# Pooled attention and maxout layers: almost all products by seven, with attention, folds and loads in one written order

## The chip, the cores and the metric

One core of a Trainium2 chip runs the whole program. The metric is the device time of one execution in microseconds (us), the median of several runs. PE is the matmul engine, DVE the vector engine, ACT the scalar engine, POOL is GpSimd, SP the engine that here only issues DMAs.

## The reference, cut to what matters

```python
# q, k, v: (8 batches, 8 heads, 576 tokens, 64)
k_p = k.reshape(B, H, 72, 8, D).mean(axis=3)          # groups of 8 keys are averaged
v_p = v.reshape(B, H, 72, 8, D).mean(axis=3)
attn = softmax(q @ k_p.T / 8)
x = (attn @ v_p) as (4608 tokens, 512)
h = max(x @ w1, x @ w2, x @ w3)                       # w1..w3: 512 x 768
out = h @ w_out                                       # w_out: 768 x 512, float32
```

Attention goes by batches (576 tokens), the layers behind it by tiles of 512 tokens, n = 0 to 8, so that a tile needs tokens of two batches.

## The kernel before, in words

**Mathematics.** Only differences from w1 are multiplied: w2-w1 and w3-w1 replace w2 and w3 (`sub_w`), and max(x w1, x w2, x w3) = x w1 + max(0, x(w2-w1), x(w3-w1)). So a tile's output is x @ wm + h @ w_out, with wm = w1 @ w_out made once (`linear`) and h = max(0, x(w2-w1), x(w3-w1)). In a normal tile the first layers (`hidden`, `hidden_part`) are 6 blocks x 2 weights x 4 pieces, 48 matmuls of 512 columns, and the output (`project`) is 4 x 10 matmuls of 512.

**By seven.** A product of 2 x 2 blocks can be had from seven block products instead of eight, with sums of blocks on both sides (Strassen's scheme in Winograd's form). `seven` does it for first layers, `out_seven` for outputs. The weights' sums (`fold_w`, `fold_out`) are made once. The sums of the tokens (T1 to T4, `fold_x`, `sums_of`) and of h (`fold_h`, `sums_of`) are made for each tile. The products are added up partly in PSUM, partly by additions on DVE after ACT has copied a product out. First layers by seven are 84 matmuls of 256 columns, outputs by seven 70 of 256. Before, tiles 6 to 8 have first layers by seven, and tiles 2, 3, 4, 7 and 8 outputs by seven; the others are normal.

**Order.** Every engine works through its instructions in the order in which the program writes them (the scheduler is switched off). Up to the end of `linear` the order is that of `block(0, ...)`: attention of batch 0, tile 0's first layers, wm. Then come project(0), tiles 1 to 4, each from a word list in `MIDDLE` (h is a piece of the first layers, a digit a product of an output, k, q, s, v, x the attention steps of the next batch), tile 5 (`block(5, LEAD, ...)`), and a woven last part, `ORDER`, with batch 7, tiles 6 to 8 and the outputs of 5 and 6 (F). `s` makes scores and their exponentials, `v` multiplies by the values and divides, `x` turns the result into xT, the layers' operand: on PE up to batch 2, by a DMA transpose from SP from batch 3 on. `T` turns a batch's q by one DMA transpose into qT.

**Folds and loads.** The sums over eight keys or values of batches 1 to 7 (but batch 1's keys, which DVE folds) are made by POOL in three steps (`fold_steps`, L161, L162, L164), and loads of k, q, v (576 KB each in the tile's type) are issued in POOL's queue. Two buffers each hold kt, vt and qb. xT is a ring of 2048 tokens.

**PSUM** has eight banks. In the middle part three are pw (first layers, outputs), two pairs are att (attention), one is tr. In the woven part there are pa, bc, po, sc and val.

Of the kernel before, what the change touches and what calls it, by code (L numbers as in the profile page):

```python
# [14 lines left out]
def kernel(  # L15
# [26 lines left out]
    NG = 9  # L42
# [22 lines left out]
    kts, vts, qbs, kps, qTs, ets = {}, {}, {}, {}, {}, {}  # L65

# [15 lines left out]
    def load_v(b, eng, dtype=F16, cuts=(0, H)):  # L82
        if b == 0:
            vts[0] = ld.tile([96, 4096], dtype, name="vt0", tag="vt")[:, 0:3072].rearrange(
                "p (h i d) -> p h i d", h=H, i=6)
            src = v[0].rearrange("h (p i) d -> p h i d", i=6)
            return [eng.dma_start(out=vts[0][:, h:g], in_=src[:, h:g])
                    for h, g in zip(cuts, cuts[1:])][-1]
        vts[b] = ld.tile([Sp, H, POOL, D], dtype, name="vt", tag="vt")
        src = v[b].rearrange("h (sp j) d -> sp h j d", j=POOL)  # L90
        return [eng.dma_start(out=vts[b][:, h:g], in_=src[:, h:g])
                for h, g in zip(cuts, cuts[1:])][-1]

    def load_q(b):
        qbs[b] = ld.tile([128, 4, NG, D], BF16, name="qb", tag="qb")
        src = q[b].rearrange("h s d -> (h s d)").rearrange(
            "(hp p t d) -> p hp t d", hp=4, p=128, t=NG)
        n = 2 if b == 0 else 4
        for i in range(0, 4, n):
            nc.gpsimd.dma_start(out=qbs[b][:, i:i + n], in_=src[:, i:i + n])  # L100
# [42 lines left out]
    vp_all = const.tile([Sp, B, H, 65], F16, name="vp", tag="vp")  # L143
# [10 lines left out]
    def fold(e, t, out, dtype=F32):  # L154
        return list(fold_steps(e, t, out, dtype))

    def fold_steps(e, t, out, dtype=F32):
        part, n = t.shape[:2]
        f = const.tile([part, n, 4, D], dtype, name="half" if dtype == F32 else "halfh",
                       tag="half" if dtype == F32 else "k16")  # L160
        yield e.tensor_tensor(out=f, in0=t[:, :, 0:4, :], in1=t[:, :, 4:8, :], op=ALU.add)  # L161
        yield e.tensor_tensor(out=f[:, :, 0:2, :], in0=f[:, :, 0:2, :],  # L162
                              in1=f[:, :, 2:4, :], op=ALU.add)
        yield e.tensor_tensor(out=out, in0=f[:, :, 0, :], in1=f[:, :, 1, :], op=ALU.add)  # L164

    def new_kp(b):
        kps[b] = sb2.tile([96, 6, D], BF16, name="kp", tag="kp")

    def fold_k(b, e, i0=0, i1=6):
        if b not in kps:  # L170
            new_kp(b)
        fold(e, kts[b][:, i0:i1], kps[b][:, i0:i1], F16 if e is nc.vector else F32)

    def fold_v(b):
        fold(nc.gpsimd, vts[b], vp_all[:, b, :, 0:D])

    def pool_v(b, h, g, tag, evac):

        pvp = psum([128, g - h, D], F32, name="pvp", tag=tag[0], bufs=tag[1])
        for i in range(6):  # L180
            nc.tensor.matmul(pvp, pick[:, i, :], vts[b][:, h:g, i, :],
                             start=(i == 0), stop=(i == 5))
        evac(out=vp_all[:, b, h:g, 0:D], in_=pvp[0:Sp])

    def turn_q(b, n0, n1, evac, tag):
# [5 lines left out]
        for n in range(n0, n1):  # L191
            nc.tensor.transpose(pqt[:, n - n0, :], qf[:, 128 * n:128 * n + 128],
# [3 lines left out]
    def keys(b, tag):  # L196
        pkt = psum([128, 3, 96], BF16, name="pkt", tag=tag[0], bufs=tag[1])
        for i in range(3):
            nc.tensor.transpose(pkt[:, i, :],
                                kps[b][:, 2 * i:2 * i + 2, :].rearrange("p i d -> p (i d)"),  # L200
                                ident[0:96, 0:96])
        return pkt

    def turn_k(b):
        pkt = keys(b, ATT if len(pools) < 3 else SC)
        for par, evac in enumerate((nc.vector.tensor_copy, nc.scalar.copy)):
            for odd in range(2):
                (evac if b > 2 else nc.vector.tensor_copy)(
# [4 lines left out]
    def score(b, h, out, tp, i0, i1):  # L213
# [4 lines left out]
        nc.tensor.matmul(out, kz_all[b % 2][f % 2][rows, h, :],  # L218
# [28 lines left out]
    def turn_x(b, c0, keep, xn, tag, evac=nc.scalar.copy):  # L247
        g0 = S * b + c0
        if b > 2:
            cut = 128 - (g0 + 128) % RING  # L250
            cuts = (keep, cut, 128) if keep < cut < 128 else (keep, 128)
            for a, z in zip(cuts, cuts[1:]):
                nc.sync.dma_start_transpose(
                    out=tokens(g0 + a, g0 + z),
                    in_=xn.rearrange("p g h d -> p (g h d)")[a:z])
            return
        pxt = psum([128, KCH, 128], F16, name="pxt", tag=tag[0], bufs=tag[1])
        for kc in range(KCH):
            nc.tensor.transpose(
# [4 lines left out]
    def values(b, c0):  # L264
        tag = (ATT0, ATT, ("val", 1))[len(pools) - 1]
        pav = psum([128, 2, 512], F32, name="pav", tag=tag[0], bufs=tag[1])
        for h in range(H):
            nc.tensor.matmul(  # L268
                pav[:, h // 4, 65 * (h % 4):65 * (h % 4) + 65],
                ets[b][:, h, c0:c0 + 128], vp_all[:, b, h, :],  # L270
# [18 lines left out]
    xns, mms = {}, []  # L289

    def do(b, steps):
# [3 lines left out]
        for name in steps.split():  # L295
            i = int(name[1:] or 0)
            if name[0] in "qQ":
                turn_q(b, *QS[i], nc.vector.tensor_copy if name[0] == "Q"
                       else nc.scalar.copy, TR)
            elif name[0] == "T":  # L300
                qTs[b] = sb2.tile([128, 2 * NG, 128], BF16, name="qT", tag="qT")
                nc.sync.dma_start_transpose(
                    out=qTs[b], in_=qbs[b].rearrange("p hp t d -> p (hp t d)"))
            elif name[0] == "k":
                turn_k(b)
            elif name[0] == "K":
                fold_k(b, nc.vector)
# [7 lines left out]
            elif name[0] == "S":  # L315
                next(out_sums, None)
# [7 lines left out]
            else:  # L324
                turn_x(b, *CHUNKS[i], xns[b, i], TR if b == 1 else ATT,
                       nc.vector.tensor_copy if name[0] == "X" else nc.scalar.copy)
# [11 lines left out]
    def turn_w(jc, evac):  # L338
        pwt = psum([128, KCH, 128], F16, name="pwt", tag=TR[0], bufs=TR[1])
        for kc in range(KCH):  # L340
            nc.tensor.transpose(pwt[:, kc, :], w_sb[0][:, kc, bass.ts(jc, 128)], identh)
        evac(out=w1T[:, jc, :], in_=pwt.rearrange("p k c -> p (k c)"))

    def linear():

        for kc in range(KCH):
            pm = psum([128, C], F32, name="pm", tag="pw", bufs=3)
            for jc in range(JCH):
                nc.tensor.matmul(pm, w1T[:, jc, bass.ts(kc, 128)], wo_sb[:, jc, :],
# [7 lines left out]
    def hidden_part(n, jc, c0, c1, hT):  # L357
        x = tokens(NB * n + c0, NB * n + c1)
        for wi in range(1, 3):
            pw = psum([128, c1 - c0], F32, name=f"pw{wi}", tag="pw", bufs=3)  # L360
            for kc in range(KCH):
                mm = nc.tensor.matmul(pw, w_sb[wi][:, kc, bass.ts(jc, 128)],  # L362
# [37 lines left out]
    def project(n):  # L400
        hT = hTs[n]
        for mm in range(4):
            m = 4 * n + mm
            last = m == TOK // 128 - 9
# [3 lines left out]
            for c in ((slice(0, C // 2), slice(C // 2, C)) if last else (slice(0, C),)):  # L408
                tag = PW if len(pools) < 3 else PA if last else PO
                po = psum([128, c.stop - c.start], F32, name="po", tag=tag[0], bufs=tag[1])  # L410
                for kc in range(KCH):
                    nc.tensor.matmul(po, tokens(128 * m, 128 * m + 128)[:, kc], wm_sb[:, kc, c],  # L412
                                     start=(kc == 0), stop=False)
                yield
                for jc in (0, 3, 1, 4, 2, 5):
                    nc.tensor.matmul(po, hT[:, jc, bass.ts(mm, 128)], wo_sb[:, jc, c],  # L416
                                     start=False, stop=(jc == JCH - 1))
                if c.start:
                    nc.vector.tensor_copy(out=osb[:, c], in_=po)
                else:  # L420
                    nc.scalar.copy(out=osb[:, c], in_=po)  # L421
                for u in range(2):
                    b, g = divmod(2 * m + u, NG)
                    dst = out[S * b:S * b + S, :].rearrange("(r g) c -> r g c", g=NG)
                    (nc.scalar if last and u else nc.sync).dma_start(
                        out=dst[:, GS[g], c], in_=osb[64 * u:64 * u + 64, c])
# [5 lines left out]
    def heat(n):  # L432
        for _ in range(n):
            nc.tensor.matmul(wm, warm[:, 0:128], warm, start=True, stop=True)
# [12 lines left out]
    def sum_k0(a, i):  # L447
        for j in range(4):
            nc.tensor.matmul(pk0[a][:, i % 3], k16[:, i, j, :], identh[0:96, 0:96],
# [67 lines left out]
    def block(n, plan, parts):  # L517

        for slot, _ in enumerate(part for stage in parts for part in stage(n)):
            for b, steps in plan.get(slot, ()):  # L520
                if b < B:
                    do(b, steps)
# [3 lines left out]
    PA, BC, PO = ("pa", 2), ("bc", 1), ("po", 1)  # L526
    FIRST = {1: (0, 0), 2: (1, 2), 7: ("S3", "T3")}
    PRODUCTS = FIRST | {3: ("S4", 3), 4: (3, "T4"), 5: ("S1", "T1"), 6: ("S2", "T2")}
    sw = {}

    LEAD = {0: [(6, "s0")], 1: [(6, "s1")], 2: [(6, "s2")], 3: [(6, "s3")],
            4: [(6, "s4")], 5: [(6, "s5")], 6: [(6, "s6")], 7: [(6, "s7")],
            8: [(6, "v0 x0")], 9: [(6, "v1 x1")]}

    def minus(out, a, b):
        gate[:] = [nc.vector.tensor_tensor(out=out, in0=a, in1=b, op=ALU.subtract)]

    def fold_w(wi):
# [3 lines left out]
        tag = ("w1T", "mw0")[wi - 1]  # L542
        s = const.tile([128, 4, 2, 128 * JH], F16, name=f"sw{wi}", tag=tag)
        sw[wi] = dict(zip(range(4), a)) | {f"S{i + 1}": s[:, i] for i in range(4)}
        nc.vector.tensor_tensor(out=s[:, 0], in0=a[2], in1=a[3], op=ALU.add)
        yield
        minus(s[:, 2], a[0], a[2])
        yield
        minus(s[:, 1], s[:, 0], a[0])
        yield  # L550
        minus(s[:, 3], a[1], s[:, 1])
        yield

    def halves(n):

        return {i: tokens(NB * n + HALF * (i % 2), NB * n + HALF * (i % 2) + HALF,
                          2 * (i // 2), 2 * (i // 2) + 2) for i in range(4)}

    def turns(n):
        return (pad3 if n % 2 else pad)[:, 0:4]  # L560

    def fold_t(e, x, t):
        for i, a, b in ((0, x[1], x[0]), (1, x[3], t[0]), (2, x[3], x[1]), (3, x[2], t[1])):
            e.tensor_tensor(out=t[i], in0=a, in1=b, op=ALU.subtract)  # L564

    def fold_x(n):

        x, t = halves(n), turns(n)
        late = n >= LAST - 1
        for part in ([slice(0, 1), slice(1, 2)] if late else [slice(0, 2)]):  # L570
            fold_t(nc.gpsimd if late else nc.vector,
                   {i: x[i][:, part] for i in x}, [t[:, i, part] for i in range(4)])
        return {f"T{i + 1}": t[:, i] for i in range(4)}

    LAST = TOK // NB - 1
    th, so_new, tt_all, gate, held = {}, [], [], [], []

    def out_w(z, r0, r1):

        i, j = divmod(z, 2)  # L580
# [399 lines left out]
```

## Time and profile before

| | us |
|---|---|
| median of 3 runs (lowest, highest) | 226.55 (226.42, 226.98) |
| the profiled execution | 228.01 |
| its span, first to last instruction | 226.3 |
| DMA transposes xT<-xn: count, median to landing | 27, 2.7 |
| qT<-qb: count, median to landing | 5, 7.0 |
| loads of k, q, v: median to landing | 8.2, 13.0, 17.5 |

The span is that of one execution taken by the profiler; busy times count overlapping instructions of one engine once, and a mean duration can be longer than the distance to the next instruction's start, since the engines overlap the end of one with the beginning of the next. Idle time of an engine costs something only where another one waits for it.

### The profile page before, as it was taken

The page shows a single profiled execution, that of the slowest core. Times are in us where ns is not written, and L with a number is a line of the kernel's source. Part 1 is how long each engine was busy: PE and PEld are TensorE (multiplying, and loading weights), DVE is VectorE, ACT ScalarE, POOL GpSimd, SP SyncE. Part 2 cuts the span into 40 slices and gives each one's busy share as a digit, 9 for nine tenths or more (in the row PEclk, how much of TensorE's full clock was granted, in tenths as well). Part 3 has the DMA queues.
Part 4 walks back from the last instruction along what each step waited for, and adds up shares of the span by engine and source line. Part 5 has one row for each costly group of instructions (what it writes and reads, how often), then busy time and mean ns, then how long its engine had stood idle before and what let it go on. Part 6 is the DMA issues. An engine that isn't in the chain of part 4 may idle for free.

```text
span 226.3 us, 4691 instructions
## 1 busy us (share of the span) xinstructions
PE 214.7 (95%) x1807; PEld 146.4 (65%) x1807; DVE 148.6 (66%) x292; ACT 122.3 (54%) x221; POOL 138.6 (61%) x111
## 2 busy tenths in 40 slices
PE   6788999999999999999999999699999999999993
PEld 2467745558656555965686568355677677788882
DVE  3668876038595385876679668535668886898840
ACT  2267524755874577238624862475687446555330
POOL 7974300999949967787677758999500913872020
PEclk9999999999999999999999999999999999999999
DMA  6999999989759999659999599965241534200265
GB/s 167 210 197 197 208 207 208 203 163 224 128 106 191 217 220 208 112 129 151 199 226 191 31 216 236 182 126 132 58 107 29 122 61 95 46 3 0 55 203 164
DMA packets 47351, 33.54 MB, mean 148 GB/s; under 512 B 27041, under 2 KB 42337, under 8 KB 47329
## 3 DMA queue, kind: packets, MB, share of 16 engines
q0 software_dynamic: 16944, 16.98, 48.1%
q1 hardware_dynamic: 29936, 15.87, 33.0%
q10 hardware_dynamic: 448, 0.39, 0.7%
q8 instruction: 14, 0.23, 0.5%
q14 instruction: 9, 0.07, 0.1%
HBM read 34.60 MB, written 9.44 MB: 195 GB/s over the span
## 4 chain that ended last, share of the span: by engine, by line
PE 69%; DMA 15%; POOL 11%; issue 1%; DVE 1%; ACT 1%; POOLq 0%
PE pw L362 21%; PE oA L713 9%; DMA vt<-in_v_dram 8%; PE pA L789 7%; PE po L416 7%; PE po L412 5%; PE oC L713 4%; PE psc L218 4%; DMA mw<-in_moe_w_dram 4%; PE pC L789 3%; POOL half L161 3%; DMA xT<-xn 3%; PE pav L268 3%; PE oB L713 2%; POOL half L162 2%; PE pB L789 2%
## 5 line engine op out<-in xcount | busy, mean ns | idle before, releaser
L362 PE MATMUL pw<-xT,mw 128*128 128x512 f16 (+1 forms) x336 | 72.8, 348 | 1.9 <-DMA xT<-xn 1.6
L362 PEld LDWEIGHTS <-mw 128*128 128x128 f16 x336 | 31.6, 98 | 22.3 <-DMA xT<-xn 1.8
L370 DVE TENSOR_TENSOR hT<-t,pw 128x512 f16<-128x512 f16 (+1 forms) x42 | 25.4, 609 | 25.1 <-ACT et L223 17.8
L223 ACT ACTIVATE et<-psc 72x576 f16<-72x576 f32 (+2 forms) x54 | 35.2, 661 | 6.8 <-PE psc L218 6.7
L161 POOL TENSOR_TENSOR half<-vt 72x2048 f32<-72x2048 f16 x7 | 28.4, 4061 | 13.8 <-DMA vt<-in_v_dram 13.3
L162 POOL TENSOR_TENSOR half<-half 72x1024 f32<-72x1024 f32 (+1 forms) x13 | 27.3, 2098 | 11.0 <-DVE rcp L274 6.1
L368 ACT ACTIVATE t<-pw 128x512 f16<-128x512 f32 (+1 forms) x42 | 22.5, 537 | 16.2 <-PE pw L362 15.8
L276 DVE TENSOR_TENSOR xn<-pav,rcp 128x512 f16<-128x512 f32 x40 | 27.7, 692 | 1.4
L416 PE MATMUL po<-mwo,hT 128*128 128x512 f16 (+1 forms) x102 | 23.5, 366 | 0.0
L218 PE MATMUL psc<-qT,kz 128*128 128x320 bf16 (+2 forms) x120 | 22.4, 278 | 0.8 <-DVE qT L194 0.6
L218 PEld LDWEIGHTS <-kz 128*128 128x128 bf16 x143 | 13.1, 98 | 13.3 <-ACT qT L194 1.1
L161 POOL TENSOR_TENSOR half<-ktFalse 96x1536 f32<-96x1536 f16 x6 | 18.7, 3125 | 4.0 <-issue 2.9
L564 POOL TENSOR_TENSOR pad<-xT 128x256 f16<-128x256 f16 x8 | 5.9, 732 | 22.5 <-ACT pad L795 13.9
L795 ACT CAST pad<-pA 128x512 f16<-128x512 f32 x27 | 15.6, 588 | 7.2 <-PE pA L789 7.0
L268 PEld LDWEIGHTS <-et 72*128 72x128 f16 x320 | 15.1, 98 | 3.6 <-issue 0.4
L723 ACT COPY osb<-oA 128x512 f32<-128x512 f32 x12 | 7.0, 586 | 19.2 <-PE oA L713 19.2
L274 DVE RECIPROCAL rcp<-pav 128x8 f32<-128x8 f32 x40 | 8.2, 204 | 14.0 <-PE pav L268 13.6
L412 PE MATMUL po<-wm,xT 128*128 128x512 f16 (+1 forms) x68 | 16.6, 366 | 0.0
L268 PE MATMUL pav<-vp,et 72*128 72x65 f16 x320 | 16.4, 194 | 0.1
L421 ACT COPY osb<-po 128x512 f32<-128x512 f32 (+1 forms) x16 | 9.2, 573 | 12.0 <-PE po L416 12.0
L789 PEld LDWEIGHTS <-sw 128*128 128x128 f16 x144 | 13.7, 98 | 2.5
L766 DVE TENSOR_TENSOR pad<-pad,pC 128x512 f16<-128x512 f16 x18 | 12.3, 685 | 3.9 <-PE pC L789 3.6
(122 smaller groups left out, 380.0 us busy)
## 6 DMA issues: line engine op xcount, KB each, us to landing
out_dram<-osb SPq DMA_DIRECT2D x38, 128.0 KB, 5.5
ktFalse<-in_k_dram POOLq DMA_DIRECT2D x7, 576.0 KB, 8.2
qb<-in_q_dram POOLq DMA_DIRECT2D x7, 576.0 KB, 13.0
vt<-in_v_dram POOLq DMA_DIRECT2D x7, 576.0 KB, 17.5
mw<-in_moe_w_dram POOLq DMA_DIRECT2D x9, 256.0 KB, 9.4
out_dram<-osb SPq DMA_DIRECT2D x8, 256.0 KB, 7.4
ktTrue<-in_k_dram SPq DMA_DIRECT2D x3, 384.0 KB, 5.2
out_dram<-ob SPq DMA_DIRECT2D x8, 128.0 KB, 2.6
```

What stands on the lines that cost most here:

```text
L161: yield e.tensor_tensor(out=f, in0=t[:, :, 0:4, :], in1=t[:, :, 4:8, :], op=ALU.add)
L162: yield e.tensor_tensor(out=f[:, :, 0:2, :], in0=f[:, :, 0:2, :], in1=f[:, :, 2:4, :], op=ALU.add)
L218: nc.tensor.matmul(out, kz_all[b % 2][f % 2][rows, h, :], qTs[b][rows, n + i0:n + i1, 64 * (h % 2):64 * (h % 2) + 64], start=True, stop=True)
L223: nc.scalar.activation(out=out, in_=in_, func=FT.Exp, scale=1.0 / 64.0)
L268: nc.tensor.matmul(pav[:, h // 4, 65 * (h % 4):65 * (h % 4) + 65], ets[b][:, h, c0:c0 + 128], vp_all[:, b, h, :], start=True, stop=True)
L276: nc.vector.tensor_tensor(out=xn, in0=pv[:, :, :, 0:D], in1=rcp.to_broadcast([128, 2, 4, D]), op=ALU.mult)
L362: mm = nc.tensor.matmul(pw, w_sb[wi][:, kc, bass.ts(jc, 128)], x[:, kc], start=(kc == 0), stop=(kc == KCH - 1))
L370: nc.vector.tensor_tensor(out=hT[:, jc, c0:c1], in0=t, in1=pw, op=ALU.max)
L412: nc.tensor.matmul(po, tokens(128 * m, 128 * m + 128)[:, kc], wm_sb[:, kc, c], start=(kc == 0), stop=False)
L416: nc.tensor.matmul(po, hT[:, jc, bass.ts(mm, 128)], wo_sb[:, jc, c], start=False, stop=(jc == JCH - 1))
L713: nc.tensor.matmul(p, left, right, stop=(r == 4), skip_group_check=True, start=(i in FIRST and r == 0 and (m == 0 or n == LAST)))
L789: mm = nc.tensor.matmul(p[:, w], a[:, kc, bass.ts(g, 128)], b[:, kc, :], start=(i in FIRST and w + kc == 0), stop=(w + kc == 2), skip_grou ...
```

## The change

- Tiles 2 to 8 now have first layers by seven, and tiles 1 to 8 outputs by seven. Tile 1's first layers are normal in products, but in halves of 256 tokens (`two_products`).
- The middle lists are gone. From the end of `linear` on, one list, `ORDER`, names every step: attention (q, k, s, v, x, T), p for project(0)'s halves, A to H for tile 1's first layers, 1a to 7c for a tile's products (three column groups a, b, c), 1d to 7d for its output products, t and u for the differences of tokens and of h, F, f, S, G for the weights' sums, K and V for pieces of key and value folds, and < for a load. A star behind a step puts its evictions on DVE instead of ACT (`move`).
- PSUM from there on: four banks that any product takes and gives back (`take`, `give`), two for scores and transposes (sc), two for values.
- Keys: DVE folds eight to two (`halfh`, `kp`), and PE adds the two while it turns them (`keys`). Values: POOL folds in six pieces per batch (28 of 72x512, 14 of 72x4x128 over all batches), and DVE makes the last addition. All differences of tokens and of h are on DVE.
- Product 1 is copied from one PSUM bank to another, so that product 2 is added up onto it there; h's first halves are then made as in normal tiles, with no additions in SBUF.
- Waits that are written by hand: a value piece on POOL waits for the last preceding DVE operation of those with two SBUF inputs (`shared`), and a load waits for the matmul ahead of it (`latest`) and for the last DMA transpose ahead of it (`turned`). The qT of batches 3 to 7 is turned in three DMA transposes each.

```diff
+    def move(out, in_):
+        (nc.vector.tensor_copy if on_vector[0] else nc.scalar.copy)(out=out, in_=in_)
...
     def keys(b, tag):
-            nc.tensor.transpose(pkt[:, i, :],
-                                kps[b][:, 2 * i:2 * i + 2, :].rearrange("p i d -> p (i d)"),
-                                ident[0:96, 0:96])
+            for j in range(2):
+                matmul(pkt[:, i, :], kps[b][:, j, 2 * i:2 * i + 2, :].rearrange("p i d -> p (i d)"),
+                                 identh[0:96, 0:96], start=(j == 0), stop=(j == 1))
...
-                nc.sync.dma_start_transpose(
-                    out=qTs[b], in_=qbs[b].rearrange("p hp t d -> p (hp t d)"))
+                turned[:] = [nc.sync.dma_start_transpose(
+                    out=qTs[b][:, 6 * i:6 * i + 6],
+                    in_=qbs[b].rearrange("p hp t d -> p (hp t d)")[:, 768 * i:768 * i + 768])]
...
+    def both(out, a, b, op, e=nc.vector):
+        t = e.tensor_tensor(out=out, in0=a, in1=b, op=op)
+        if e is nc.vector:
+            shared[:] = [t]
...
+        if i == 1:
+            move(out=bank("B", n, g), in_=p)
+        elif i in (6, 5):
+            move(out=y[:, i == 5], in_=p)
+        elif i in (2, 3):
+            t0 = sb2.tile([128, NB], F16, name="t0", tag="t0")[:, 0:HALF]
+            nc.scalar.activation(out=t0, in_=p[:, 0], func=FT.Relu)
+            nc.vector.tensor_tensor(out=h_of(g)[:, i - 2], in0=t0, in1=p[:, 1], op=ALU.max)
+        if i in (5, 7) and (n, 12 - i, g) in done:
+            plus(1)
+        if i == 4:
+            plus(0)
+            shared[:] = [nc.vector.scalar_tensor_tensor(
+                out=h_of(g + JH), in0=y[:, :, 0], scalar=0.0, in1=y[:, :, 1],
+                op0=ALU.max, op1=ALU.max)]
...
+        f = const.tile([Sp, H, 4, D], F32, name="half", tag="half")
+        for i in range(0, H, 2):
+            c = slice(i, i + 2)
+            yield e.tensor_tensor(out=f[:, c], in0=t[:, c, 0:4, :], in1=t[:, c, 4:8, :],
+                                  op=ALU.add)
+        for i in range(0, H, 4):
+            c = slice(i, i + 4)
+            yield e.tensor_tensor(out=t[:, c, 0:2, :], in0=f[:, c, 0:2, :], in1=f[:, c, 2:4, :],
+                                  op=ALU.add)
+        both(vp_all[:, b % 3, :, 0:D], t[:, :, 0, :], t[:, :, 1, :], ALU.add)
...
+            elif name[0] == "<":
+                load = {"k": load_k, "v": load_v, "q": load_q}[name[1]](
+                    int(name[2]), *([nc.gpsimd] if name[1] != "q" else []))
+                after([load], latest[0])
+                if turned:
+                    after([load], turned[0])
...
+    SEVEN = (2, 3, 4, 5, 6, 7, 8)
...
+    ORDER = """
+        q12* V1 q13 p s10 V1 F <k3 V1 V1 s11 G F V1 F p s12 V1 s13 p s14 p K2 q20 V2 K2 s15
+        p <k4 s16 V2 V2 V1 s17 s18 q21 <v3 k2 G v10 p v11 x10 s20 x11* V2 q22 v12 s21 F H3
+        s22 s23 V2 v13 E3 x12* q23 V2 v14 A3 G K3 x13 D3 K3 s24 <q3 V2 <q4 s25 <k5 K4 E4 f
+        s26 T3 T3 K4 B3 G s27 s28 C4 V3 D4 v20 x14 V3 A4 k3 p V3 k4 v21 S t1 T3 f C3 T4 T4
...
+    """
```

More of the change, by code (lines that the diff above doesn't have):

```diff
@@ L205, in turn_k @@
         pkt = keys(b, ATT if len(pools) < 3 else SC)
-        for par, evac in enumerate((nc.vector.tensor_copy, nc.scalar.copy)):
+        for par in range(2):
             for odd in range(2):
-                (evac if b > 2 else nc.vector.tensor_copy)(
+                move(
                     out=kz_all[b % 2][par][64 * par:64 * par + 64, :, 0:Sp].rearrange(
@@ L407, in project @@
             osb = two[:, mm % 2]
[L408 to L426, printed above, removed]
+            po = take(("p", mm), (128, C))
+            for kc in range(KCH):
+                matmul(po, tokens(128 * m, 128 * m + 128)[:, kc], wm_sb[:, kc],
+                                 start=(kc == 0), stop=False)
+            yield
+            for jc in (0, 3, 1, 4, 2, 5):
+                matmul(po, hT[:, jc, bass.ts(mm, 128)], wo_sb[:, jc],
+                                 start=False, stop=(jc == JCH - 1))
+            move(out=osb, in_=po)
+            give(("p", mm))
+            for u in range(2):
+                b, g = divmod(2 * m + u, NG)
+                dst = out[S * b:S * b + S, :].rearrange("(r g) c -> r g c", g=NG)
+                nc.sync.dma_start(out=dst[:, GS[g]], in_=osb[64 * u:64 * u + 64])
             yield
@@ L527, with give @@
+    def give(key):
+        free_banks.append(taken.pop(key)[0])
     FIRST = {1: (0, 0), 2: (1, 2), 7: ("S3", "T3")}
     PRODUCTS = FIRST | {3: ("S4", 3), 4: (3, "T4"), 5: ("S1", "T1"), 6: ("S2", "T2")}
[L529 to L536, printed above, removed]
@@ L559, in turns @@
[L559 to L573, printed above, removed]
@@ L846 @@
[L846 to L867 removed]
+        return wo_sb[:, JH * j:JH * j + JH, c] if h else wm_sb[:, 2 * j:2 * j + 2, c]
@@ L945 @@
+    """
+    run(ORDER)
+    last = out_last(LAST)
+    for i in range(4):
+        sum_h(LAST, i)
     for i, m in ((1, 0), (1, 1), (2, 0), (2, 1), (6, 0), (6, 1), (7, 0), (5, 0), (5, 1),
                  (7, 1), (3, 0), (3, 1), (4, 0), (4, 1)):
-        outs(i, m)
-    for _ in tiles:
-        pass
+        last(i, m)
 _INS = ['q', 'k', 'v', 'moe_w1', 'moe_w2', 'moe_w3', 'moe_w_out']
```

688 lines of the change are left out of this document (312 added, 376 removed), and 3 rows, old and new, of the table stop.

## Prediction

> **What bounds the kernel now.** I read the page's head first, then the stretches (us of the stretch, then each engine's busy time and count), then the chain that ended last (start, length), then the timelines of single engines where the change puts work. "Slot" below means the distance from start to start of instructions that follow each other without a wait; the page's durations are longer, since the next one starts before the last has ended.
>
> ```profile
> span 226.3 us, 4691 instructions
> PE 214.7 (95%) x1807; PEld 146.4 (65%) x1807; DVE 148.6 (66%) x292; ACT 122.3 (54%) x221; POOL 138.6 (61%) x111
> ```
>
> ```profile
> 58.00:158.00 100.00, 97.40 (x768) 61.56 (x766) 65.06 (x130) 57.23 (x100) 78.60 (x44) 1.00 0.97 167
> 158.00:220.00 62.00, 62.00 (x552) 48.97 (x551) 47.27 (x82) 34.67 (x66) 23.11 (x28) 1.00 0.32 70
> ```
>
> ```profile
> 78.72 2.59 PE pw L362 x12
> ...
> 134.97 1.09 PE oB L713 x10
> ...
> 138.71 6.32 DMA xT<-xn
> ```
>
> PE is busy 95% of the span; in the two long stretches it is busy 97.4 of 100 and 62.0 of 62 us, at a granted clock of 1.00. The chain gives its slots: 12 matmuls of 512 columns in 2.59 us are 0.216 us each; 10 of 256 columns in 1.09 are 0.109, so half the columns cost half the time and the smaller products lose nothing. From 37.5 us, where the weight product wm ends, to PE's end at 222.5, I sum the slots to 178.1 us; the other 6.9 are idle: 2.8 of it between 134 and 146, behind the one DMA transpose of the last line, 1.4 between 43 and 58, some 0.4 in each middle tile, 0.7 in 158 to 220. So PE's work sets the time, and waits only a little.
>
> **The seven products (PE).** A normal tile's first layers are 48 matmuls of 512 columns, 10.37 us; by seven they are 84 of 256, 9.16. Tiles 2 to 5 change: 4 x 1.21 = 4.8 us less. A normal tile's output is 40 x 0.216 = 8.64; by seven 70 x 0.109 = 7.63. Tiles 1, 5 and 6 change: 3.0 less. Tile 1's first layers are now 96 matmuls of 256 columns instead of 48 + 24 of 512: no difference. The keys are now added up by PE: 42 matmuls in place of 21 transposes of 0.042, 0.9 more. The score pieces of batches 1 to 6 cut the same columns otherwise: nothing. Sum: 7.0 us less, 171.1 in place of 178.1. The built order has 588 and 560 such matmuls, so the count itself is certain.
>
> **What moves to the vector engine.** Its slots:
>
> ```profile
> 62.08 1.26 POOL L164 TENSOR_TENSOR vp<-half 72x512 f16<-72x512 f32 x1
> ...
> 62.28 1.35 DVE L597 TENSOR_TENSOR so<-wm 128x512 f16<-128x512 f16 x1
> ...
> 64.00 0.42 DVE L597 TENSOR_TENSOR so<-wm 128x512 f16<-128x512 f16 x1
> 64.34 0.42 DVE L597 TENSOR_TENSOR so<-wm,so 128x512 f16<-128x512 f16 x1
> 64.67 0.68 DVE L370 TENSOR_TENSOR hT<-t,pw 128x512 f16<-128x512 f16 x1
> 65.27 0.55 DVE L597 TENSOR_TENSOR so<-mwo 128x768 f16<-128x768 f16 x1
> 65.86 0.56 DVE L597 TENSOR_TENSOR so<-so,mwo 128x768 f16<-128x768 f16 x1
> 66.33 0.55 DVE L545 TENSOR_TENSOR sw<-mw 128x768 f16<-128x768 f16 x1
> ```
>
> These give 0.60 for a 512-wide operation that reads PSUM (64.67 to 65.27), 0.47 for 768 and 0.33 for 512 columns of float16 in SBUF. Counted in the built order: 42 additions onto ys for 27 onto pad, +9.1; 3 more final maxima, +1.8; 32 token differences xs where 16 were there (tiles 7 and 8 had theirs on POOL), +5.4; 32 differences of hT for some 18, +6.8; key folds of six more batches at 0.87 + 0.50, +7.6; seven last steps of the value folds, +3.1; evictions by `move` (marked with a star), +7.2; output additions +1.2; key copies that went to ACT, -6.8. That is +35: from 135.5 us of slots (the page's 148.6 without overlaps) to about 171. Some 25 of that stands before 37.5, as now. From there on DVE has 146 us of work against PE's 171, or 85%, where it has 66% between 158 and 220 (47.27 busy less 0.08 for each of 82 instructions, 40.7 of 62); by stretches of 6 us of PE's work it stands between 3.6 and 6.3, and no queue of more than 1.3 us builds up by these sums. So it stays hidden, but with little room.
>
> Three costs aren't in the trace. The copy of product 1 from bank to bank in PSUM (26 on ACT, 2 on DVE): the nearest row is osb<-oA, 586 ns; the far end is the 1020 ns of a 1024-wide activation; I take the near one, since ACT gets to about 120 us of slots and has room in either case. The key fold's second step, 96x768 to a turned layout: between 0.47 (768 columns in order) and 0.95 (the 1536-wide first step); I take 0.50, 0 to 3 us in all. The value fold's last addition: 0.33 to 0.69, taken at 0.45, 0 to 2 us. All are hidden as long as DVE is.
>
> **POOL and its queue.** POOL loses the key folds and the differences (63 us) and keeps 42 value pieces, 28 x 1.02 + 14 x 1.17 = 45 us; it is idle most of the time. But each load from batch 3 on now waits, in POOL's queue, for the matmul ahead of it and for the last DMA transpose; behind it stand value pieces, behind these the last addition, now in DVE's queue, and behind that every eviction (rival B). On SP, 15 thirds of qT at some 1.2 us of issue stand in place of five wholes at 1.95 to 5.5, and stores queue behind them as now; a staging tile osb is wanted again only a tile later (some 20 us), so late stores are hidden up to that.
>
> **DMA transposes.** Now:
>
> ```profile
> L253 SPq DMA_TRANSPOSE xT<-xn x8: 1192/1232/1497, 120.7 to 148.2; - x8
> ...
> DMA to landing us min/median/max: 2.3/6.8/11.2
> ```
>
> Between 120 and 150 us they land up to 11.2 us after issue (after 158, without loads, 2.4 in the median). The one issued at 122.06 landed at 133.14, the key load of 122.33 at 132.98: it stood still until the load was in. Before, the first reader of a tile's last transposes stands 2.7 to 5.9 us of PE work behind; that is the 2.8 us of idle. In the new order the nearest reader beside loads is 6.4 us away (one qT third), most 8 to 20, and after the last load (PE's work at 121) 4.1 to 8.9. So the 2.8 goes. What is late next are the thirds of qT of batches 3 and 4: loads q3, q4, k5 stand just ahead of them, and the free queue lands one every 2.8 to 3.8 us (32.7, 35.6, 39.3, 42.1, 45.1, 48.6), which puts the first third at about 69.5, and its reader at 70: no wait, or 1 to 2 us.
>
> **Ends.** Up to 37.5 the two kernels are the same. v1 lands at 39.3 and its fold needs 4 x 1.02 + 2 x 1.17 + 0.45 and a load's 0.55, to about 47; PE has 8.5 us of work till then from 37.5, so 1 us of idle stays there. At the end the last stores are two of 128 KB one behind the other on SP (0.62 each to issue, 2.6 at most to landing) in place of two 64 KB ones on SP and ACT: +1.0 on the present 3.8.
>
> **Sum.** 37.5 + 171.1 + idle + 4.8 = 213.4 + idle. Idle: at least 1.9 (the 0.7 in 62 us of the late stretch, over 171), at most about 10; I take 4.5: 1 at the start of batch 1 and 3.5, or 2%, after it, since DVE is fuller than in that stretch. Span 217.9. The profiled execution took 228.01 with a span of 226.3, 1.7 around it; the median of the runs is 226.55, 1.46 below that execution. So 217.9 + 1.7 = 219.6 for such an execution, 218.1 as median; the idle's bounds give 215.5 to 223.6, and mostly up to 221.
>
> **Rival A: faster by less, the port.** In the fence above, DVE's 0.42 us addition at 62.28 took 1.35: it ended 0.28 after POOL's vp fold ended (63.34). With 42 POOL pieces between some 110 such DVE operations, about 15 pieces stand in the order with the next one closer than their own length: up to 10 us of DVE's time, of which PE sees what exceeds the 0.5 to 1 us that DVE has spare in 6 us. Price 3 to 7 us: 221 to 225.8. Against it: a piece waits for the DVE operation before it, and most have 1.2 to 3 us free behind them. The Trainium skill, "SBUF — State Buffer", section "Who interferes with whom", says that a vector instruction with two SBUF inputs and a GpSimd one that reads SBUF exclude each other, and the later waits for the whole of the other; by that rule, the trace agrees (1.35 for 0.42).
>
> **Rival B: slower, a late load stops DVE.** Now a late key or value load holds up POOL alone (POOL waited 13.3 us for v1 while PE ran on). After, the key folds and the last value additions stand in DVE's queue, and evictions behind them, so PE stops within the 0.6 to 1 us that its banks buffer. From issue to fold there are 10 to 15 us of PE work (k4 11.2, k5 13.5, k6 13); now k takes 8.2, q 13.0 and v 17.5 us to land in the median, and 20.1 at worst. If loads that wait for transposes, and transposes that stand still for loads, push that to 16 to 18 us in the new order, each of three to five rounds costs 3 to 5 us: 218.1 + 10 to 18 = 228 to 236. It decides from a sum of 8.5 us on. For it: DMA is the busiest resource from 58 to 158 (share 0.97). Against it: three loads at once make up the present 17.5, the new order spreads them, and the free queue needs 3.3 each.
>
> **Chances.** Forecast (215 to 221) 0.60; A 0.16; B 0.20; near the old time 0.03; below 215 0.01. A measurement of this kernel can tell about 0.3%, 0.7 us. So faster 0.77, same 0.03, slower 0.20. The range that leaves out B's upper part and the lowest end is 214.5 to 226.5.
>
> **What would show it.** Right: PE's slots about 171 after 37.5, PE over 96% from 58 us on, DVE near 187 us busy as the page counts, no chain piece of a DMA transpose over 1 us. Wrong in A's way: two-input DVE rows well over 0.42 and 0.55. Wrong in B's way: halfh<-ktFalse or vp<-vt on DVE with idle before them that ends with a DMA or POOL, or PE waits for qT. If PE is under 92% between 58 and 158, the forecast is wrong.

## The result, and the profile after

The changed kernel takes 234.79 us (median of 4 runs, 233.71 to 237.24) where the kernel before takes 226.66 (226.42 to 226.98): 1.034 times as long, with a 95% interval of 1.030 to 1.038. The profiled execution took 234.6 us, 1.7 around a span of 232.9. Medians here and below hold all executions; the ratios leave out those more than 1.5% longer than the fastest of their kernel.

Head of the page of the changed kernel:

```profile
span 232.9 us, 5417 instructions
PE 211.0 (91%) x2117; PEld 172.7 (74%) x2118; DVE 191.6 (82%) x379; ACT 138.9 (60%) x283; POOL 83.1 (36%) x90
```

Its stretches, as they were shown of before:

```profile
58.00:158.00 100.00, 90.90 (x986) 79.15 (x985) 86.34 (x179) 71.21 (x152) 38.53 (x37) 1.00 1.03 155
158.00:220.00 62.00, 60.94 (x596) 53.42 (x594) 56.24 (x108) 31.59 (x64) 7.49 (x6) 1.00 0.37 76
```

PE's work did shrink: from 37.5 us to PE's end its slots sum to 170.35 us, 7.8 less than before. But PE is busy for 90.9 of the 100 us in which loads run, not 97.4; behind them, it is nearly full. PE ends at 227.75, the stores 5.1 later. So the span's 6.6 us are 7.8 off the slots, 13.0 more idle (19.9, was 6.9) and 1.3 more tail.

Of the chain that ended last (start, length), the pieces of DMA from 52 us on, and the vp between two of them; the rest is PE's, but for short pieces of DVE, ACT and SP:

```profile
66.51 7.96 DMA qT<-qb
...
91.78 7.30 DMA qT<-qb
...
111.30 14.71 DMA xT<-xn
...
126.43 0.43 DVE vp L535
...
130.10 3.67 DMA out_dram<-osb
```

Before, one such piece stood there, of 6.32 us. These are DMA transposes, from issue to landing, and one store that stood behind them. The waits (who, for what: us in total, times, longest) say whom they stopped:

```profile
POOL half L805 <- DMA vt<-in_v_dram: 30.4, 5, 12.3
...
DVE xs L535 <- DMA xT<-xn: 3.5, 4, 1.7
ACT osb L78 <- DMA out_dram<-osb: 3.3, 1, 3.3
PE psf L70 <- DMA qT<-qb: 3.2, 2, 2.3
```

The first line is the longest of the four and sets no time: no piece of POOL stands in the chain. The other three are PE's: directly, or through a DVE or ACT queue with PE's evictions in it. How the longest piece comes about is seen in POOL's timeline (start, length of the issue) beside SP's:

```profile
104.91 0.55 POOL L92 DMA_DIRECT2D ktFalse<-in_k_dram  x1 [6.20 <-PE pb L70]
...
107.68 0.85 POOL L104 DMA_DIRECT2D vt<-in_v_dram  x1
108.52 0.77 POOL L112 DMA_DIRECT2D qb<-in_q_dram  x1
109.28 0.54 POOL L92 DMA_DIRECT2D ktFalse<-in_k_dram  x1
```

```profile
105.90 8.18 SPq L254 DMA_TRANSPOSE xT<-xn  x3
123.41 1.27 SPq L303 DMA_TRANSPOSE qT<-qb  x1
124.77 3.15 SPq L254 DMA_TRANSPOSE xT<-xn  x1
```

Four loads (k6, v6, q6, k7) leave within 4.9 us and land at 111.05, 118.49, 123.35 and 126.00. The xT transpose issued at 111.30 lands at 126.007, 7 ns after the last of them (landings are those that the trace gives for each DMA). From 114 to 123.4 SP issues nothing: its next transpose, a third of qT of batch 6, waits for q6, and the stores of finished tiles wait behind it until 128. So at 125 PE stands 1.8 us for the xs and vp behind xT, and at 131 2.6 us for an output tile whose old content had not left.

### The profile page after: what moved, and what is told of

Read it like the earlier page. It is cut to its first block, busy times and chain, and to the rows that moved or that the text cites. A ratio compares the mean times of both kernels' runs of the same rounds, so it can differ in the third digit from the quotient of the medians.

```text
span 232.9 us, 5417 instructions
## 1 busy us (share of the span) xinstructions
PE 211.0 (91%) x2117; PEld 172.7 (74%) x2118; DVE 191.6 (82%) x379; ACT 138.9 (60%) x283; POOL 83.1 (36%) x90
## 4 chain that ended last, share of the span: by engine, by line
PE 67%; DMA 17%; DVE 7%; ACT 4%; issue 1%; SPq 1%; DVEq 0%; ACTq 0%
PE pb L70 48%; DMA qT<-qb 7%; DMA xT<-xn 6%; PE psf L70 5%; PE pw L70 4%; PE pav L70 3%; DMA ktTrue<-in_k_dram 3%; PE pm L70 2%; DMA out_dram<-osb 2%; DVE xn L277 1%; ACT et L224 1%; PE pqt L74 1%; DVE xs L535 1%; PE oC L70 1%; PE pxt L74 1%
## 5 line engine op out<-in xcount | busy, mean ns | idle before, releaser
L805 POOL TENSOR_TENSOR half<-vt 72x512 f32<-72x512 f16 x28 | 34.0, 1233 | 37.8 <-DMA vt<-in_v_dram 30.4
L224 ACT ACTIVATE et<-psf 72x512 f16<-72x512 f32 x63 | 36.0, 595 | 6.4 <-PE psf L70 6.1
L70 PE MATMUL pb<-xT,mw 128*128 128x256 f16 x264 | 36.6, 272 | 2.1 <-DVE hT L644 0.7
L634 DVE TENSOR_TENSOR ys<-ys,pb 128x512 f16<-128x512 f16 x42 | 28.4, 680 | 3.6 <-ACT ys L78 2.5
L78 ACT CAST ys<-pb 128x512 f16<-128x512 f32 x36 | 21.1, 587 | 8.3 <-PE pb L70 5.3
L70 PE MATMUL psf<-qT,kz 128*128 128x256 bf16 (+4 forms) x161 | 22.7, 249 | 3.8 <-DMA qT<-qb 3.2
L70 PE MATMUL pb<-xs,sums 128*128 128x256 f16 x126 | 24.1, 272 | 0.3 <-ACT et L224 0.3
L70 PE MATMUL pb<-xs,sw 128*128 128x256 f16 x126 | 24.0, 272 | 0.0
L70 PE MATMUL pb<-mwo,hT 128*128 128x256 f16 (+1 forms) x120 | 19.3, 294 | 0.0
L70 PE MATMUL pb<-soh,hs 128*128 128x256 f16 x138 | 19.2, 273 | 0.0
```

The lines of the kernel that those rows point to most:

```text
L70: latest[0] = nc.tensor.matmul(*args, **kw)
L78: (nc.vector.tensor_copy if on_vector[0] else nc.scalar.copy)(out=out, in_=in_)
L224: nc.scalar.activation(out=out, in_=in_, func=FT.Exp, scale=1.0 / 64.0)
L634: nc.vector.tensor_tensor(out=y[:, j], in0=y[:, j], in1=bank("C", n, g), op=ALU.add)
L805: yield e.tensor_tensor(out=f[:, c], in0=t[:, c, 0:4, :], in1=t[:, c, 4:8, :], op=ALU.add)
```

## The experiments

The theory after the result was: loads and DMA transposes hold each other up, and PE waits for what the transposes bring ("DMA"). The rivals were: POOL's pieces hold up DVE ("port"); DMA has too much to do wherever it stands ("amount"); the places in the engines' queues ("queues"). PE's idle from 37.5 us on, in us, counted matmul by matmul (this way before has 6.4, after 19.6). "No gate" is the run in which loads don't wait for the last DMA transpose; about 2.8 us of its column are no waiting but matmuls at a granted clock of 0.50, from 48.98 to 52.39 and from 107.3 to 110.43 (an estimate: what their slots take beyond the usual ones):

| stretch | before | after | no loads | no transposes | no loads, no folds | no gate | loads by order |
|---|---|---|---|---|---|---|---|
| 37.5-53 | 0.8 | 3.8 | 4.4 | 4.6 | 3.2 | 5.1 | 4.6 |
| 53-90 | 1.1 | 2.4 | 1.1 | 1.6 | 1.0 | 1.3 | 1.6 |
| 90-112 | 0.5 | 3.7 | 1.5 | 2.1 | 0.9 | 8.2 | 1.5 |
| 112-134 | 0.5 | 5.8 | 0.6 | 0.6 | 0.6 | 0.9 | 0.8 |
| 134-170 | 2.9 | 2.5 | 1.5 | 0.6 | 0.7 | 0.6 | 0.8 |
| 170-end | 0.6 | 1.5 | 1.1 | 1.1 | 1.1 | 1.2 | 1.1 |
| time | 226.7 | 234.8 | 224.8 | 226.1 | 221.9 | 232.5 | 225.9 |

**No loads.**

```
             elif name[0] == "<":
-                load = {...}[name[1]](int(name[2]), ...)
-                after([load], latest[0])
-                if turned:
-                    after([load], turned[0])
+                tiles = {"k": kts, "v": vts, "q": qbs}[name[1]]
+                tiles[int(name[2])] = tiles[2 - int(name[2]) % 2]
```

> Leaves out the loads of k, q and v for batches 3 to 7 (the tiles of batches 1 and 2 are used again, so the later batches attend to other data); every other instruction stays. In the trace of the changed kernel PE idles 19.9 us from 37.5 us on: 3.8 up to 53, 1.7 at 68 to 78, 3.3 at 90 to 100, 5.3 at 122 to 134, 1.9 at 158 to 170. Theory DMA (transposes stand still beside loads, and PE waits for them): the idle of 68 to 134 goes, some 10 us, 223 to 226 us. Rival port (DVE and POOL shut each other out; the waits for transposes only stand where DVE is late anyway): at most 3 us go, 231 or more.

Measured: 224.81 us (224.29 to 224.94), 0.989 of before (0.983 to 0.995). The landing of the xT transposes between 58 and 158, first of the changed kernel, then without loads:

```profile
DMA to landing us min/median/max: 2.3/5.2/15.1
```

```profile
DMA to landing us min/median/max: 2.3/2.4/4.3
```

Without loads a transpose takes 2.4 us, and the idle of 90 to 134 goes from 9.5 to 2.1. That fits theory DMA.

**No transposes**: the other half of the pair taken away, with the loads left in (the x of batch 3 is still turned by DMA). With the transposes goes the loads' wait for them.

```
             elif name[0] == "T":
-                ...
+                qTs[b] = qTs[2 - b % 2]
...
-            for a, z in zip(cuts, cuts[1:]):
+            for a, z in zip(cuts, cuts[1:]) if b == 3 else ():
```

> Leaves out the DMA transposes from batch 4 on and those of q of batch 3 (old contents of xT, and qT of batches 1 and 2, are used again); loads and stores stay. Theory DMA (loads and transposes hold each other up): loads land closer together, the burst k6 v6 q6 k7 in some 16 us in place of 21, nothing waits for a transpose, and the time comes near that without the loads: 224 to 227 us. Rival loads (the loads and their places in POOL's queue cost the time, whatever stands beside them): 231 to 235 us.

Measured: 226.07 us (225.22 to 227.36), 0.997 of before (0.995 to 1.000), as theory DMA had it. The same four loads land at 105.3, 111.8, 114.3 and 117.0: the last three 2.4 to 6.5 us apart, in place of 2.6 to 7.4, the last 12.2 us after its issue in place of 16.7. So it isn't the loads alone: either half of the pair taken away brings the time within 1.3 us of the other.

**The same cut in the kernel before**, as a control (its loads of batches 3 to 7 replaced by `tiles[b] = tiles[2 - b % 2]`):

> The kernel BEFORE without its loads of k, q and v of batches 3 to 7 (the tiles of batches 1 and 2 are used again): the control for the same cut in the changed kernel, which gave 224.8 us. Theory DMA (the kernel before hardly waits for its loads): its idle of 6.9 us holds one wait of 2.7 us for transposes, so 223 to 226 us. Rival bandwidth (any kernel here is some 10 us quicker without the loads, and the changed kernel is no more tied to them): 215 to 219 us.

Measured: 226.22 us (226.01 to 226.46), 0.998 of before (0.996 to 1.000), 0.2 above what theory DMA had. The kernel before gains nothing to speak of where the changed one gains 10 us. Bandwidth as such isn't what was lost.

**No value folds on POOL.**

```
-        for i in range(0, H, 2):
-            ...
-        for i in range(0, H, 4):
-            ...
+        for i in range(6):
+            yield
```

> Leaves out POOL's 42 value pieces (DVE's last addition takes two unfolded rows, so the values are wrong); loads and transposes stay. DVE's operations are 13.0 us longer in sum than their usual durations in the changed kernel, 11 of it beside POOL pieces, most at 39 to 48 and 161 to 166. Theory DMA: only the idle of the start and of 158 to 170 shrinks, 2 to 5 us: 230 to 233. Rival port: 8 or more go: 224 to 227.

Measured: 233.08 us (229.49 to 234.14), 1.017 of before (1.005 to 1.029), just above theory DMA's range and far from the rival's: the folds are not the main cost while the loads stand. The long wait is still in this run's chain, without one value piece on POOL:

```profile
107.56 14.02 DMA xT<-xn
```

**No loads and no folds**, both edits together:

> Leaves out the loads of k, q and v of batches 3 to 7 and the 42 POOL pieces that fold the values. It asks what the 10.5 us of idle after 37.5 us are that stay without the loads. Theory port (POOL's pieces hold up DVE, 7.7 us of lengthened DVE work there): 219 to 222 us. Rival queues (the order of the evictions on ACT and DVE, at the start of batch 1 above all): no more than 1.5 us less than without the loads alone, 223 to 225 us.

Measured: 221.86 us (221.77 to 222.02), 0.978 of before (0.973 to 0.983). That is 2.9 us less than without the loads, more than the rival allowed and within theory port's 219 to 222: so the port has a price, about 3 us. What DVE's instructions take beyond the usual time of their own form falls from 7.7 to 1.9 us; in the changed kernel it is 13.0, before 3.4. The row with the highest price of any run comes from the run with respread loads below, where two value pieces had been put side by side. DVE's timeline, then POOL's:

```profile
121.19 0.68 DVE L725 TENSOR_TENSOR osb<-osb,pb 128x512 f32<-128x512 f32 x1
121.78 4.98 DVE L535 TENSOR_TENSOR hs<-hT 128x768 f16<-128x768 f16 x1
126.80 0.56 DVE L535 TENSOR_TENSOR hs<-hT,hs 128x768 f16<-128x768 f16 x1
```

```profile
120.76 0.86 POOL L104 DMA_DIRECT2D vt<-in_v_dram  x1 [4.59 <-PE pb L70]
121.64 2.27 POOL L805 TENSOR_TENSOR half<-vt 72x512 f32<-72x512 f16 x2
123.87 2.47 POOL L809 TENSOR_TENSOR vt<-half 72x512 f16<-72x512 f32 x2
```

A subtraction of 0.55 us that starts just behind the first of four POOL pieces ends 0.4 us after the last of them (126.34), 4.4 us late; PE stood 4.0 us at 123.6. The Trainium skill, "SBUF — State Buffer", section "Who interferes with whom", has the later instruction wait for the whole of the other one; here it waited for four in a row.

**Transposes on PE instead**, two tries: the 25 chunks of x of batches 3 to 7 (four transposes by PE and an eviction each, four words behind the values), or the thirds of qT (six by PE and an eviction).

```
# x on PE, in turn_x; each step is put off by four words
-        if b > 2:
-            ...
-            return
# q on PE, four words ahead of the first, third and fifth score piece of its batch
-                turned[:] = [nc.sync.dma_start_transpose(...)]
+                turn_q(b, 6 * i, 6 * i + 6, move, SC)
```

> The 25 chunks of xT of batches 3 to 7 are turned on PE and evicted by ACT, four steps of the list after their values, instead of by 27 DMA transposes; the loads stay. PE gets 100 transposes of 0.055, 5.5 us more. Theory DMA: the waits for xT (about 8 of the 19.9 us of idle, with the stores behind them) go, and qT's come earlier: 229 to 233 us. Rival port: nothing goes, 238 to 241.

> The qT of batches 3 to 7 is turned on PE, in three pieces each close to its scores, and evicted by ACT, instead of by 15 DMA transposes. PE gets 90 transposes of 0.055, 5.0 us more. Theory DMA: waits for qT (1.7 at 73 and 2.4 at 97) go, those for xT stay or shrink: 233 to 238 us. Rival port: 238 to 240.

Measured: 241.01 us (240.06 to 241.48) and 234.06 (232.58 to 235.16), 1.061 (1.054 to 1.067) and 1.030 (1.023 to 1.038) of before. The first comes out at its rival's number (238 to 241), but not for its rival's reason: the long DMA waits of 112 to 134 did go, and the time went up all the same: 5.4 us of new PE work, and waits of the next kind, of this run:

```profile
PEld L74 <- DVE xn L272: 12.7, 20, 1.4
...
PE pxt L74 <- DVE xn L272: 7.1, 15, 1.1
```

PE's new transposes stand behind xn, at the end of a DVE queue that is busy 79% of the span; PE waited there 15 times, 7.1 us in all, and with the new work that costs more than the DMA transposes did. The second has 3.8 us less idle for its 4.9 us of new PE work, and ends where it began; that is within theory DMA's 233 to 238, but so is the changed kernel itself, so it decides nothing. The first doesn't speak for theory DMA, though not against it either: it brought a cost that neither theory had counted.

**Respread loads** (k5, v5, v6 and k7 at other places of ORDER, the folds behind them):

```
- <q4 s25 <k5 K4 ... t1 T3 f C3 ... 2c <v5 u4 ... t1 V5 t2 s48 ... t4 <k6 V5 2a ... 2b V5 6b 7a <v6 s53 <q6 <k7 3a
+ <q4 s25 K4 ... t1 T3 <k5 f C3 ... 2c u4 ... t1 t2 s48 ... t4 <v5 <k6 2a ... 2b 6b 7a s53 <q6 3a
- 1c V5 6d v42 6c V5 2c V5 u4 7c K6 V6 K6 V6 5d ... T6 V6 7d v43 3d <q7 3c ... 5d K7 s60 ... s64 <v7
+ 1c V5 V5 6d v42 <v6 6c V5 V5 2c V5 V5 u4 7c K6 K6 5d ... T6 7d v43 3d <q7 <k7 3c ... 5d s60 ... s64 K7 <v7
```

> The changed kernel with the loads at other places of the written order: k5 behind the last third of qT of batch 3, v5 beside k6, v6 behind chunk 2 of batch 4, k7 beside q7, and the folds of k7, v5 and v6 moved behind them; no work is left out. Theory DMA (the transposes stand still beside loads, and PE waits for what they bring): the waits at 68-78 (1.7 us), 90-100 (3.3 us) and 122-134 (5.3 us) shrink to some 0.6, 1.4 and 1: 234.8 less 7.3, 226 to 230 us. Rival amount (the transfers are too many for the queues wherever they stand): the idle comes back at other places, 233 us or more.

Measured: 238.2 us (234.35 to 239.41), 1.039 of before (1.028 to 1.050): the expectation of theory DMA missed, and the rival's number met. The waits at 68 to 78 and 90 to 100 did shrink (1.7 to 0.6, 3.3 to 0.7), but 112 to 146 grew by 4.7: v5 in front of k6 made k6 land at 115.9, as DVE waited for it; the stall of 4.98 us shown above; q7 and k7, moved beside six transposes, held five of these until 145.5 and later. By this run alone "amount" would have been the better reading. The next two say otherwise.

**No gate**: the loads don't wait for the last transpose.

```
                 after([load], latest[0])
-                if turned:
-                    after([load], turned[0])
```

> The loads no longer wait for the last DMA transpose in front of them in the order, only for their tiles, the latest matmul and their turn in POOL's queue. Rival gate (this wait pushes loads together, and they would land in time without it): 228 to 231 us. Theory DMA (a load that starts beside transposes only moves the place where they stand still): 232 to 238 us, and the transposes that were issued just ahead of a load land 5 us or more later than in the changed kernel.

Measured: 232.47 us (230.38 to 232.97), 1.023 of before (1.016 to 1.030), within theory DMA's bounds. The table shows what the gate had done: with it, the idle stands at 112 to 134; without it there is 0.9 there, and 8.2 at 90 to 112 (some 1.5 of it the lower clock), where k6, now issued at 97.5, holds the last third of qT of batch 5 (of this run's chain):

```profile
98.99 8.32 DMA qT<-qb
```

The other three loads still leave together, at 102.84, 103.68 and 104.45: they stand side by side in the order. What the gate had added was k6.

**Loads by order**: no gate, k6 behind that third, v6 just behind q6, k7 beside q7.

```
- ... s50 t4 <k6 V5 2a 6a 1b s51 s52 u3 ... 7a <v6 s53 <q6 <k7 3a ... v43 3d <q7 3c ... 5d K7 s60 ... s64 <v7
+ ... s50 t4 V5 2a 6a 1b s51 s52 <k6 u3 ... 7a s53 <q6 <v6 3a ... v43 3d <q7 <k7 3c ... 5d s60 ... s64 K7 <v7
```

> Without the wait of the loads for the last DMA transpose, as in the run without that gate (232.5 us), and with k6 issued behind the last third of qT of batch 5, k7 beside q7 instead of beside q6, and the folds of k7 moved behind that; no work is left out. Theory DMA: the wait of PE for the third of qT at 102 (5.3 us, 7.8 in the stretch 100-112) goes to under 1.5 and nothing takes its place: 225 to 228 us. Rival amount (the transfers are too many wherever they stand): the idle comes back at 112-146, 231 us or more.

Measured: 225.87 us (225.01 to 229.05, 10 runs), 0.998 of before (0.995 to 1.001), as theory DMA had it. All the work is done in this run; its stretch with loads:

```profile
58.00:158.00 100.00, 98.42 (x1081) 87.03 (x1079) 92.14 (x193) 76.63 (x162) 44.87 (x43) 1.00 1.04 162
```

PE 98.42 of 100 where it was 90.90, at the same DMA share, 1.04 for 1.03. The transposes land no sooner than in the changed kernel (median 4.9 us for xT and 5.7 for qT, for 5.2 and 5.2): many still land late, but not those that PE is next to want: in this run no engine's wait of over 0.15 us ends with one. That rules "amount" out, and gives 9 us of the 13 back.

**Two tries at the start of batch 1**, on top of that order: three weight sums of DVE moved out of it; or the keys of batch 2 moved back and evicted on DVE.

```
- V1 V1 s11 G F V1 F p ... k2 G v10 p v11 x10 s20 x11* ... s23 V2 v13
+ V1 V1 s11 F V1 p ... k2 v10 p v11 F x10 s20 G x11* ... s23 G V2 v13
# the second
- <v3 k2 G v10 p v11 x10
+ <v3 G v10 p v11 k2* x10
```

> As the run before it, and three weight sums of DVE (the third of F, the first two of G) moved out of the start of batch 1, behind its first values, so that the folds of k2 no longer stand behind them beside POOL's value pieces. Theory port (there, DVE's additions of 0.55 us take 1.4 to 2.9 beside POOL's pieces, and PE waits for what stands behind them): 2 to 3 us less than the run before it, since the granted clock of 0.6 to 0.8 after the wait goes as well. Rival (ACT's evictions set the start of batch 1): under 0.7 us less.

> The order of loads of the run that gave 225.9 us, and in it the keys of batch 2 (word k2) behind its neighbours p and v11 and evicted on DVE instead of ACT; no work is left out. In that run PE stood 1.76 us at 47.2 for the folds of k2 on DVE, and 0.88 at 51.6 for ACT behind the four key copies. Theory (these two waits are only a matter of places): 2 to 2.5 us less, 223 to 224 us, faster than the kernel before by about 1%. Rival (another wait of DVE or ACT takes their place): 225 to 226.5 us.

Measured: 227.48 us (224.84 to 229.39), 0.997 of before (0.993 to 1.001), and 230.57 (228.79 to 230.77), 1.017 (1.014 to 1.019). Neither gained: the first comes out where its rival put it, the second above both of its ranges. In the first the fold of k2, now first in DVE's queue, waited for k2's load until 45.4 and then took 2.47 us beside POOL; in the second PE, freed of k2, waited at the same place, 47.4, for DVE's last value addition (1.69 us), which stands behind the same folds. The second shows something else. Its two stretches, then those of the run it started from (PEclk is the third number from the end):

```profile
47.00:50.00 3.00, 1.21 (x16) 0.77 (x15) 2.89 (x5) 1.35 (x3) 2.75 (x2) 0.98 0.85 219
50.00:53.00 3.00, 3.00 (x22) 1.81 (x21) 1.18 (x3) 0.58 (x1) 2.99 (x4) 0.50 0.49 78
```

```profile
47.00:50.00 3.00, 1.41 (x22) 0.98 (x22) 2.89 (x6) 1.66 (x4) 2.88 (x2) 1.00 0.83 210
50.00:53.00 3.00, 2.20 (x23) 1.36 (x22) 1.62 (x4) 2.91 (x6) 2.99 (x4) 1.00 0.58 90
```

The second lost 4.7 us against the run that it started from; an estimated 2.7 of them are matmuls at a granted clock of 0.50, which its trace has from 49.90 to 53.31 and from 56.73 to 60.14.

No version that does all the work beats the kernel before by more than a measurement can tell.

## Why the prediction was wrong

- **PE's work.** Forecast 171.1, measured 170.35. Right, as was the step from 0.216 to 0.109 us.
- **The tail.** Forecast 4.8, measured 5.1.
- **DVE's load.** Forecast 187 us busy, measured 191.6. From 58 to 158 us it was busy 86.3 of 100, so the work that "stays hidden, but with little room" did stay hidden where nothing was late. At the start of batch 1 it did not have the room: from 38 to 44 us DVE was busy 5.96 of 6.
- **Idle: the step that failed.** "I take 4.5", with an upper bound of "about 10"; it was 19.9. Some 9 of the 15 that are missing (what the run with loads by order gains) lie in the sentence "In the new order the nearest reader beside loads is 6.4 us away (one qT third), most 8 to 20 ... So the 2.8 goes"; what is left is mostly the start of batch 1 and the port, below. The distances were counted in PE's work of the built order, and set against landing times of before. Two things were not worked out. The loads were taken to be spread ("the new order spreads them, and the free queue needs 3.3 each"), while the order has v6, q6 and k7 side by side, and the wait for the last transpose, which the same text names, held k6 until 104.3, just ahead of them (it left at 104.9, and at 97.5 without that wait); and beside transposes each of the four took up to 7.4 us. The transpose issued behind them at 111.30 landed with the last load, after 14.7 us, more than most of the distances. And "late stores are hidden up to" 20 us left out that SP's queue stops for a third of qT that waits for q6: 2.6 us.
- **The thirds of qT of batch 3.** "No wait, or 1 to 2 us": the first landed at 74.5 where 69.5 was forecast, its reader stood at 73.3 where 70 was; PE waited 1.1. Right by luck, both were late together.
- **The start of batch 1.** "1 us of idle stays there": 3.8, and still 3.2 with neither loads nor folds. Here the forecast looked at v1 alone, and not at the chain on DVE (weight sums, folds of k2, value addition) and ACT (evictions) that stands there. What of it is ACT's and what is DVE's wasn't separated by a run; with neither loads nor folds ACT is busy 5.80 of the 6 us from 44 to 50 and DVE 3.42, which points to ACT for the part that stays.
- **Rival A** had its mechanism right, its price at the lower bound ("3 to 7 us"): about 3 us by the run without loads and folds. It wasn't what decided.
- **Rival B** gave 228 to 236 with a chance of 0.20, and is what happened, by the cause it named ("loads that wait for transposes, and transposes that stand still for loads"), though not by its victims. The key folds and value additions in DVE's queue hardly waited for their own loads; PE waited for qT, DVE for xT, ACT for stores. Of the signs it listed, "PE waits for qT" and PE "under 92% between 58 and 158" (90.9) came true, and so did a chain piece of a transpose over 1 us. The chance was too low since it was argued from loads with "10 to 15 us" from issue to fold; the shorter distances, those of the transposes, were counted under the forecast.

## What to carry to other kernels

Where loads and DMA transposes run beside each other, count for each transpose which loads may be in flight when it is issued, and plan with the landing of the last of them, or up to 4 us behind it; a distance to the reader in compute time means nothing without this. A wait that keeps loads off transposes can push one load beside the next ones: without it, and with k6, v6 and k7 at other places of the order, the time fell by 9 us, more than the 7.8 us of PE's work that the change saves. Here, with 4% less of PE's work, waits that a few us had hidden came to light together, so the idle was the term to size, not the work.

## What the runs showed of the hardware

Without loads, an xT transpose lands 2.4 us after its issue (median). In the changed kernel 21 transposes were issued with loads in flight, and each landed between 0.5 us ahead of the last of those loads and 4.2 us behind it, up to 15.1 us after its issue. Loads issued later did not hold one up there: the transpose of 105.90 landed at 113.06, 2.0 behind k6, while v6, q6 and k7, issued 1.8 to 3.4 us after it, landed at 118.49 to 126.00. It is no strict rule: without the gate, the transpose issued at 104.80, 0.4 us behind k7, landed at 116.98 and k7 at 122.47.

Nor did a late transpose stand still all the time. Behind the one of 111.30 and its successor of 112.76, with no other DMA of SP's issued until 123.41, the trace has no 256-byte packet in SP's queue from 111.30 to 115.2, and 651 packets of loads; from 115.2 to 123.24 it has 974 of them, beside those of the loads. The Trainium skill, "DMA: Bandwidth & Descriptors", section "Queues, rings and completion order", says that each engine serves the queues it has work for in turn, packet by packet. The second stretch agrees with that; the first 3.9 us, in which only loads moved, do not. Why is not shown; what the runs show is that either half of the pair, taken away, frees the other.

Five runs have a granted clock of 0.50 for 3.41 us just behind PE's wait at 47 to 49 us. That wait was 0.96 us in the first try at the start of batch 1, 1.15 without the gate, 1.35 with q on PE, 1.58 with respread loads and 1.69 in the second try. The clock stayed at 1.00 after waits of 1.35 without loads, 1.59 with loads by order, 1.61 without transposes and 1.74 with x on PE. So the length of the wait doesn't decide. The Trainium skill, "TensorE: Matmul & The Clock Gate", section "Part 1: The HAM clock gate", describes a window that runs freely, so that the same pause may or may not halve the clock; these nine rows agree with that. It costs at most what it halves, 1.5 us of the 3 from 50 to 53 in the rows above. The spread of the run with loads by order (225.0 to 229.1) is not explained by it: its executions of 227.1, 227.6 and 229.05 us had mean granted clocks of 0.997 to 0.999, and one of 226.17 had 0.989. What makes that spread is open.
